# A two-layer mixture of experts behind a linear-attention scan: VectorE's order at five points, and gate products stored with the slot tile innermost

## The chip, the cores and the metric

The kernel runs on one core of a Trainium2 chip. The metric is device time in microseconds (us), the median of several executions; one further execution is profiled, and every row below comes from that one. The engines are named as in the profile: PE is TensorE (matmuls), PEld its weight loads, DVE is VectorE, ACT is ScalarE, POOL is GpSimd, SP only issues DMAs. A name with a q behind it (DVEq, ACTq) is that engine's sequencer, which handles waits, branches and register loads.

## What is computed

A gated linear recurrence over 4 x 768 positions gives a matrix x of 3072 tokens by 384. Two mixture-of-experts layers follow, both of this form (the second adds a bias per modality to the logits):

```python
logits = x @ w_gate
expert_idx = np.argmax(logits, axis=1)
probs = np.exp(logits - logits.max(-1, keepdims=True))
probs /= probs.sum(-1, keepdims=True) + 1e-09
gate_w = probs[np.arange(N), expert_idx]
for e in range(E):                      # 8 experts
    mask = expert_idx == e
    h = np.maximum(x[mask] @ w1[e], 0.0)          # 384 -> 1024
    out[mask] = gate_w[mask, None] * (h @ w2[e])  # 1024 -> 384
```

## The kernel before

After the attention the kernel works in two stages, one for each expert layer. The tokens are sorted by expert into slots of 128 tokens; a slot tile (below: a tile) is one such slot, and a stage has at most MT = 31 of them. In the profiled execution stage 1 runs tiles 0 to 26 and stage 2 runs tiles 0 to 24. Tiles from 24 on stand in branches that are taken only if the tile exists ("rest" branches); the first few tiles of each stage (2 and 4) are done ahead of the full table and end in a branch too.

One tile j is made of steps, each a closure with a name. For q = 0 to 3, `g1_q` is 18 matmuls of 128 columns (gathered tokens against a quarter of w1, each value split into a high and a low f16 part), `hh_q` is ACT's relu to f16, `hl_q` is DVE's low part (relu minus `hh_q`), and `g2_q` is 6 matmuls of 384 columns, of which every third needs `hl_q`. `ev` makes the output scale, `yo` is ACT's scaled output and POOL's scatter DMA. Beside them stand steps for later tiles: `sq` and `sv` scale the tokens of tile j+2 (ACT's square; then a chain of four DVE operations, L775 to L778, output `xs`), `T`, `xh`, `xl` transpose and split those of tile j+1, and in stage 1 `la` to `ld` make the logits of the second layer.

Where the expert changes, the new weights are split into f16 parts in place: ACT makes `wh` (L746), DVE `wl` (L747), in eight pieces of 128x768. A piece is named by h or l, the layer 0 or 1 and the quarter: `l11` is DVE's low part of w2's second quarter. Each stands in a branch that is taken where the expert changes; below, a tile where that happens is a split tile.

The order of all this is not left to a scheduler. A table POS gives every step of a tile a position (0 to 10, one number line for all engines), CHG does the same for the weight pieces (a position from 10 on means: in the next tile, 10 less), and EXT gives the steps that occur once per stage (position 23.74 is tile 2, 3.74). Steps are sorted by position and issued in that order, so each engine runs its instructions in the order of these numbers.

The routing is turned into slots by `finishing`, `tabling` and `gating`. `gating` (`gate1` and `gate2` in EXT, for the two stages) has four steps: ACT's exponential; DVE's sum, reciprocal, split of the gate into two f16 numbers and two products AQ = A x gate (A is the mask, 31 slot tiles by nt token tiles); on PE one matmul for each of the nt token tiles (24 in stage 1, 31 in stage 2) with AQ of that token tile as moving operand, 62 columns; and DVE's reading of the result, which gives each tile its scale and its token numbers.

Of the kernel before, what the change touches and what calls it, by code (L numbers as in the profile page):

```python
# [9 lines left out]
F16 = mybir.dt.float16  # L10
# [3 lines left out]
ALU = mybir.AluOpType  # L14
# [5 lines left out]
P = 128  # L20
# [5 lines left out]
NT = N // P  # L26
# [78 lines left out]
def attention(tc, ctx, C, q, k, v, a_re, a_im, wg, flags, emit_y, emit_lg, extra, ps, inp):  # L105
# [266 lines left out]
MT=31; MS=32; WF=544  # L372
# [4 lines left out]


POS=[dict(r1=-1.031,g1_0=0,hh_0=0.547,g1_1=0.882,hl_0=1.39,la=2.05,hh_1=2.196,g1_2=2.293,g2_0=2.443,lc=2.732,hl_1=3.114,r2=4.038,hh_2=4.156,T=4.338,
    g2_1=4.65,xh=4.8,hl_2=4.8,xl=5.173,sq=5.3,g1_3=5.65,hh_3=5.721,lb=5.802,g2_2=6.338,sv=6.511,lt=6.833,ga=6.883,ev=7.217,hl_3=7.445,ld=7.7,  # L380
    g2_3=8.105,yo=9.966),
    dict(la=-2.149,ga=-2.099,r1=-1.063,g1_0=-0.801,g1_1=-0.106,hh_0=1.2,hh_1=2.2,hl_0=2.367,hl_1=2.614,g1_2=2.928,T=3.282,r2=3.634,g2_0=3.64,lc=3.664,
    hh_2=4.688,xh=4.798,hl_2=4.8,xl=5.2,g1_3=5.366,sq=5.443,lb=5.487,g2_1=5.99,hh_3=6.083,hl_3=7.1,ev=7.3,g2_2=7.5,lt=7.586,ld=7.7,sv=7.978,g2_3=8.5,
# [4 lines left out]
    dict(h00=1.25,l00=2.555,h01=3.772,l01=3.889,h10=5,l10=5.85,h02=6.908,h11=7.334,l02=7.573,h03=8.381,l11=8.43,l03=9.238,h12=11.713,h13=12.469,l12=12.6,  # L388
    l13=13.5)]

EXT=dict(ga1=[9.894],tab1=[10.675,11.888,14.575,16.434,19.076],sc2=[14.852,16.409],tu2=[17.791,18.391,19.266],
    sc3=[16.942,20.231],gate1=[13.14,22.34,23.74,26.94],bias=[38.314],guess=[7.193,9.387],ec=[1.828,2.259,3.158],es=[5.811,7.12,9.347],eg0=[-0.314],
    eg1=[2.518],eg2=[2.797],eg3=[0.24],esc0=[7.854,8.86],esc1=[9.262,9.598],esc2=[17.6,18.2],esc3=[17.787,19.2],etu0=[10.7,10.819,11.2],etu1=[16.719,
    16.834,17.692],etu2=[20.882,21.035,21.741],etu3=[26.7,26.797,29.053],wsp=[0.41],lgl=[1.567,2.117,4.049,5.381,7.217],bat=[11.965,12.932,13.065,
    16.165],fin2=[15.779,17.6,18.5,21.1,21.3],ga2=[21.761],tab2=[18.791,23.611,24.661,26.111,28.111],scE=[31.762,31.857],tuE=[34.33,34.944,35.562],
    scF=[34.804,36.2],gate2=[33.763,38.234,40.083,40.999],ckw=[5.75,7.75],ck=[8.464])


HINT=1.5; DRAIN=6.9
# [33 lines left out]
class Router:  # L433
# [89 lines left out]
    def gating(s, pool, ps):  # L523

        tmp,sign,q,A,bm,T,gscale=s.late
        nc=s.tc.nc; C=s.C; nt=s.nt; nm=s.name
        K=lambda shape,n_,dt=F32: pool.tile(shape,dt,name=nm+n_,bufs=1)

        def once(f):
            def g(shape,n_,dt=F32):  # L530
                if n_ not in s.made: s.made[n_]=f(shape,n_,dt)
                return s.made[n_]
            return g
        K,T=once(K),once(T)
        sm,g2,dl,ig,iv=(T([P,w],n_) for n_,w in (("sm",nt),("g2",nt),("dl",nt),("ig",MT),("iv",MT))); mp=T([P,2*MT],"mp"); AQ=K([P,2,MT,nt],"AQ",F16)
        sg,val,ab=(K([P,MT],n_) for n_ in ("sg","val","ab")); ids=K([P,MT],"ids",I32)
        ex=T([P,nt,E],"ex"); nc.scalar.activation(ex,s.d,AF.Exp)
        yield
        g=s.gate; nc.vector.tensor_reduce(out=sm,in_=ex,op=ALU.add,axis=AX.X)
        nc.vector.tensor_scalar(out=sm,in0=sm,scalar1=1e-9,scalar2=None,op0=ALU.add)  # L540
        nc.vector.reciprocal(g,sm)
        if sign is not None:
            nc.vector.tensor_mul(g2,g,sign); g=g2
        nc.vector.tensor_copy(q[:,1,:],g)
        nc.vector.tensor_sub(dl,g,q[:,1,:])
        nc.vector.tensor_scalar(out=q[:,2,:],in0=dl,scalar1=1024.0,scalar2=None,op0=ALU.mult)
        for j in (1,2): nc.vector.tensor_tensor(out=AQ[:,j-1],in0=A,in1=bm(q[:,j,:]),op=ALU.mult)
        yield
        pm=ps.tile([P,512],F32,name="pm")
        for i in range(nt):  # L550
            nc.tensor.matmul(pm[:,:2*MT],s.boh[:,i,:],AQ[:,:,:,i],start=(i==0),stop=(i==nt-1))
        yield
        nc.vector.tensor_copy(mp,pm[:,:2*MT])
        s.sg,s.val,s.ab,s.ids=sg,val,ab,ids
        nc.vector.scalar_tensor_tensor(s.sg,mp[:,MT:],1.0/1024,mp[:,:MT],op0=ALU.mult,op1=ALU.add)
        nc.vector.tensor_scalar(out=s.val,in0=s.sg,scalar1=0.0,scalar2=None,op0=ALU.not_equal)
        if sign is not None: nc.scalar.activation(s.ab,s.sg,AF.Abs,scale=gscale)
        else: nc.vector.tensor_scalar(out=s.ab,in0=s.sg,scalar1=gscale,scalar2=None,op0=ALU.mult)
# [130 lines left out]
class Rot:  # L689
# [10 lines left out]
class Bufs:  # L700
# [48 lines left out]
class Stage:  # L749
# [98 lines left out]
    def tile(s, j, mid=(), old=None, chg=None, refill=False, **kw):  # L848


        W=s.W
        st=[(s.pos[k],f) for k,f in s.steps(j,**kw).items()]

        for k,p in s.chg.items():
            c=old if p>=10 else chg
            if c is None: continue
            def part(c=c,k=k):
                with s.tc.If(c["hl".index(k[0])]!=0): W.split(((int(k[1]),int(k[2])),),**{"lo" if k[0]=="h" else "hi":False})  # L858
            st.append((p%10,part))
        if refill:  # L860
            rf=s.refill(j-1)
            for k in ("r1","r2"): st.append((s.pos[k],lambda: next(rf)))
        st.extend(mid)
        st.sort(key=lambda t:t[0])
        for _,f in st: f()
# [194 lines left out]
def attention__moe__moe2_kernel(tc, q, k, v, a_re, a_im, w_gate, w1, w2, mid, w_gate2, mbias, out):  # L1060
    nc=tc.nc
    with ExitStack() as ctx:
# [8 lines left out]
        W=Weights(tc,cst)  # L1071
# [62 lines left out]
        with ExitStack() as mctx:  # L1134
# [31 lines left out]
            def logits(j, yo):  # L1166

                st=isinstance(j,int)
                px=rt.tile(); y=yo()
                for d in range(ND): nc.tensor.transpose(px[:,d*P:(d+1)*P],y[:,d*P:(d+1)*P],C.ident)  # L1170
                yield
                xT=bf.lxT.tile(); nc.scalar.copy(xT.rearrange("p d t -> p (d t)"),px[:,:DM])
                yield
                own=not st or j>=NL; pl=None
                if own:
                    pl=rt.tile()
                    for d in range(ND): nc.tensor.matmul(pl[:,:E],xT[:,d,:],wg2s[:,d,:],start=(d==0),stop=(d==ND-1))
                else:
                    xTs[j]=xT
                    if j%4==3: grp[0]=group(j-3)  # L1180
                p=(j-3)%4 if st and 3<=j<NL+3 else 3
                if p<3: next(grp[0])
                yield
                if p==0: next(grp[0])
                yield
                if own:
                    js=slice(j,j+1) if st else bass.ds(j,1)
                    nc.vector.tensor_tensor(out=R2.lg[:,js,:].rearrange("p o e -> p (o e)"),in0=pl[:,:E],in1=bias[:,js,:].rearrange("p o e -> p (o e)"),op=ALU.add)
                if p in (1,2): next(grp[0])
                elif st and p==3 and 3<j<NL+3: next(grp[0])  # L1190
                yield
# [6 lines left out]
            H1,H2={},{}  # L1198
            def put(H, nm, f, t=0):

                it=[]
                def step():
                    if not it: it.append(f())
                    next(it[0],0)
                for k in EXT[nm]:
                    j,k=divmod(k+.5,10); H.setdefault(t+int(j),[]).append((k-.5,step))
            def one(f):
                def g():
                    f(); yield
                return g  # L1210
# [9 lines left out]
            for i in range(EK):  # L1220
                put(H1,f"eg{i}",one(lambda i=i: S2.gather(i,exg[i],R2.eids[:,i:i+1])),EN+5)
                put(H1,f"esc{i}",lambda i=i: S2.scaling(i,eev[i],exs[i]),EN+5)
                put(H1,f"etu{i}",lambda i=i: S2.turning(i,exh[i],exl[i]),EN+5)
            put(H2,"wsp",one(lambda: W.split(((1,2),(1,3)))))
            put(H2,"lgl",lambda: logits(S1.last(),lambda: S1.ylast)); put(H2,"bat",lambda: R2.batch(NL,MT-NL,sb,rt,{},imv))
            put(H2,"fin2",lambda: R2.finishing(sb,sb,rt,1.0/(WS*WS),R1.idf))
            put(H2,"ga2",one(lambda: [S2.gather(EK+i) for i in range(3)]))
# [5 lines left out]
            ck=Check(tc,sb,cst,C,fl,W,R1,R2)  # L1233
# [97 lines left out]
```

## Time and profile before

| | |
|---|---|
| median of the timed executions | 791.32 us (790.51 to 792.84, 3 runs) |
| the profiled execution's own time | 784.05 us |
| its span, first to last instruction | 782.3 us |
| mean granted TensorE clock in it | 0.973 |
| PE busy | 730.2 us (93%) |
| DVE busy | 533.9 us (68%) |
| ACT busy | 474.5 us (61%) |
| POOL busy | 297.9 us (38%) |

Times in the rows are counted from the start of the span. A timeline row gives the start, the duration, the engine, the line, the operation, the tile that it writes and those that it reads, a count where rows are merged, and in square brackets how long the engine sat idle before it and who ended that. Matmuls overlap: a matmul row's duration includes the time in the pipeline, so the pace is read from the starts. The clock 1.00 is 2.4 GHz and 0.50 is 1.2 GHz.

### The profile page before, as it was taken

The numbers are of one execution on the slowest core, as the hardware profiler recorded it, in microseconds if no ns is written. First come the engines' busy times: TensorE is split into PE (matmuls) and PEld (weight loads), VectorE is DVE, ScalarE is ACT, GpSimd is POOL, SyncE is SP. The second block draws the span as 40 slices with busy tenths as digits, with TensorE's granted clock in tenths as the row PEclk, the third lists the DMA queues.
The fourth block names the chain that finished last, engine by engine and source line by source line (L and its number), as shares of the span: only waits on it lengthen the run. The fifth ranks groups of instructions, "written<-read, shape, count | busy, mean of one in ns | idle before, by whom it ended". The sixth has DMA issues, their size and how long they took to land. (4 is left out here: it accounts for less than half of the span.)

```text
span 782.3 us, 23431 instructions
## 1 busy us (share of the span) xinstructions
PE 730.2 (93%) x8451; PEld 587.4 (75%) x8451; DVE 533.9 (68%) x1415; ACT 474.5 (61%) x1007; POOL 297.9 (38%) x289
## 2 busy tenths in 40 slices
PE   7688999899899989999999999999899999999994
PEld 2367878787788867878777878788777878878873
DVE  7888898899789978474747586764564435445354
ACT  7799989798687426374746565675432436434452
POOL 5657788577575231222232224221121222222221
PEclk9799999899899999999999999999999999999997
DMA  9979777675231342433525162524033111611111
GB/s 211 221 146 214 174 153 165 118 173 102 62 82 62 98 158 79 165 112 126 165 91 176 61 197 82 194 68 170 19 112 125 59 47 43 222 43 43 63 42 30
DMA packets 159261, 91.40 MB, mean 117 GB/s; under 512 B 131804, under 2 KB 149764, under 8 KB 159104
## 3 DMA queue, kind: packets, MB, share of 16 engines
q1 hardware_dynamic: 151872, 68.49, 34.1%
q0 software_dynamic: 7232, 21.05, 8.8%
q8 instruction: 71, 1.16, 0.6%
q14 instruction: 86, 0.70, 0.3%
HBM read 192.54 MB, written 20.84 MB: 273 GB/s over the span
## 5 line engine op out<-in xcount | busy, mean ns | idle before, releaser
L823 PEld LDWEIGHTS <-wh 128*128 128x128 f16 x1296 | 127.6, 98 | 10.8 <-ACTq L888 3.0
L824 PEld LDWEIGHTS <-wh 128*128 128x128 f16 x1296 | 127.6, 98 | 8.2 <-issue 1.4
L825 PEld LDWEIGHTS <-wl 128*128 128x128 f16 x1296 | 127.6, 98 | 0.0
L844 POOL DMA_INDIRECT x<-yo,r1ids x27 | 31.7, 1174 | 181.8 <-ACT yo L843 125.0
L747 DVE SCALAR_TENSOR_TENSOR wl<-ws,wh 128x768 f16<-128x768 f32 x88 | 83.6, 962 | 13.1 <-ACTq L858 7.2
L746 ACT ACTIVATE wh<-ws 128x768 f16<-128x768 f32 x88 | 74.1, 844 | 8.9 <-ACTq L858 5.1
L836 PE MATMUL mpu<-wh,hl 128*128 128x384 f16 x216 | 70.5, 327 | 5.0 <-DVE hl L828 4.3
L836 PEld LDWEIGHTS <-hl 128*128 128x128 f16 x432 | 42.2, 98 | 42.3 <-DVE hl L828 11.8
L836 PE MATMUL mpy<-wh,hl 128*128 128x384 f16 x216 | 70.7, 327 | 2.5 <-DVE hl L828 1.6
L844 POOL DMA_INDIRECT out_dram<-yo,r2ids x21 | 21.0, 1002 | 130.9 <-ACT yo L843 123.8
L834 PE MATMUL mpy<-wh,hh 128*128 128x384 f16 x216 | 70.7, 327 | 0.0
L835 PE MATMUL mpy<-wl,hh 128*128 128x384 f16 x216 | 70.6, 327 | 0.0
L834 PE MATMUL mpu<-wh,hh 128*128 128x384 f16 x216 | 70.4, 326 | 0.0
L835 PE MATMUL mpu<-wl,hh 128*128 128x384 f16 x216 | 70.4, 326 | 0.0
L823 PE MATMUL mpk<-xh,wh 128*128 128x128 f16 x384 | 68.4, 220 | 1.3 <-ACTq L888 1.3
L823 PE MATMUL msc<-xh,wh 128*128 128x128 f16 x384 | 67.6, 219 | 1.3 <-DVEq L888 1.3
L825 PE MATMUL mpk<-xh,wl 128*128 128x128 f16 x384 | 68.4, 220 | 0.0
L824 PE MATMUL mpk<-xl,wh 128*128 128x128 f16 x384 | 68.4, 220 | 0.0
L825 PE MATMUL msc<-xh,wl 128*128 128x128 f16 x384 | 67.6, 219 | 0.0
L823 PE MATMUL mpq<-xh,wh 128*128 128x128 f16 x384 | 67.6, 219 | 0.0
L824 PE MATMUL mpq<-xl,wh 128*128 128x128 f16 x384 | 67.6, 219 | 0.0
L825 PE MATMUL mpq<-xh,wl 128*128 128x128 f16 x384 | 67.6, 219 | 0.0
(512 smaller groups left out, 2230.9 us busy)
## 6 DMA issues: line engine op xcount, KB each, us to landing
ws<-in_moe_w_dram SPq DMA_DIRECT2D x100, 1536.0 KB
ar<-in_a_re_dram SPq DMA_DIRECT2D x24, 192.0 KB
ai<-in_a_im_dram SPq DMA_DIRECT2D x24, 192.0 KB
k<-in_k_dram SPq DMA_DIRECT2D x24, 192.0 KB
q<-in_q_dram SPq DMA_DIRECT2D x24, 192.0 KB
v<-in_v_dram SPq DMA_DIRECT2D x24, 192.0 KB
x<-zero SPq DMA_DIRECT2D x8, 576.0 KB
x<-yt SPq DMA_DIRECT2D x24, 192.0 KB
```

What stands on the lines that cost most here:

```text
L746: nc.scalar.activation(H_,S_,AF.Copy,scale=WS,accum_out=s.fl[:,s.n:s.n+1]); s.n+=1
L747: if lo: nc.vector.scalar_tensor_tensor(L_,S_,WS,H_,op0=ALU.mult,op1=ALU.subtract)
L823: nc.tensor.matmul(o,W.h1[:,d,fs],x.h[:,d,:],start=(d==0),stop=False)
L824: nc.tensor.matmul(o,W.h1[:,d,fs],x.l[:,d,:],start=False,stop=False)
L825: nc.tensor.matmul(o,W.l1[:,d,fs],x.h[:,d,:],start=False,stop=(d==ND-1))
L834: nc.tensor.matmul(o,hh[:,r,:],W.h2[:,f,:],start=(f==0),stop=False)
L835: nc.tensor.matmul(o,hh[:,r,:],W.l2[:,f,:],start=False,stop=False)
L836: nc.tensor.matmul(o,hl[:,r,:],W.h2[:,f,:],start=False,stop=(f==NF-1))
L844: nc.gpsimd.indirect_dma_start(out=s.dst,out_offset=bass.IndirectOffsetOnAxis(ap=R.ids[:,j:j+1] if ids is None else ids(),axis=0),in_=y,in ...
```

## The change

Five points of the order are moved, and the layout of AQ is turned round. In stage 1 `hl_3` goes from 7.445 to 6.45, ahead of `sv` (6.511). The piece `l11` goes, in tiles from 23 on, to position 11.5, that is 1.5 of the next tile; its code for stage 2's first expert then stands in `wsp`, which also takes its two `wl` operations from 0.41 of stage 2's tile 0 to 2.7. The last two steps of stage 1's table (`tab1`) go from 16.434 and 19.076 to 15.6 and 16.42. The last three steps of stage 2's gates (`gate2`) go from 38.234, 40.083 and 40.999 to 42.65, 46.05 and 46.6, so out of tile 3 and the beginning of tile 4 into the middle of tile 4. AQ was stored as [2, 31, nt], the token tile innermost; it becomes [nt, 2, 31], so DVE writes it with a step of 62 elements, and each matmul reads 62 neighbouring elements.

```diff
...
-    g2_1=4.65,xh=4.8,hl_2=4.8,xl=5.173,sq=5.3,g1_3=5.65,hh_3=5.721,lb=5.802,g2_2=6.338,sv=6.511,lt=6.833,ga=6.883,ev=7.217,hl_3=7.445,ld=7.7,
+    g2_1=4.65,xh=4.8,hl_2=4.8,xl=5.173,sq=5.3,g1_3=5.65,hh_3=5.721,lb=5.802,g2_2=6.338,sv=6.511,lt=6.833,ga=6.883,ev=7.217,hl_3=6.45,ld=7.7,
...
+LATE=dict(l11=11.5)
...
-    scF=[34.804,36.2],gate2=[33.763,38.234,40.083,40.999],ckw=[5.75,7.75],ck=[8.464])
+    scF=[34.804,36.2],gate2=[33.763,42.65,46.05,46.6],ckw=[5.75,7.75],ck=[8.464])
...
-        sm,g2,dl,ig,iv=(T([P,w],n_) for n_,w in (("sm",nt),("g2",nt),("dl",nt),("ig",MT),("iv",MT))); mp=T([P,2*MT],"mp"); AQ=K([P,2,MT,nt],"AQ",F16)
+        sm,g2,dl,ig,iv=(T([P,w],n_) for n_,w in (("sm",nt),("g2",nt),("dl",nt),("ig",MT),("iv",MT))); mp=T([P,2*MT],"mp"); AQ=K([P,nt,2,MT],"AQ",F16)
...
-        for j in (1,2): nc.vector.tensor_tensor(out=AQ[:,j-1],in0=A,in1=bm(q[:,j,:]),op=ALU.mult)
+        for j in (1,2): nc.vector.tensor_tensor(out=AQ[:,:,j-1,:].rearrange("p n m -> p m n"),in0=A,in1=bm(q[:,j,:]),op=ALU.mult)
...
-            nc.tensor.matmul(pm[:,:2*MT],s.boh[:,i,:],AQ[:,:,:,i],start=(i==0),stop=(i==nt-1))
+            nc.tensor.matmul(pm[:,:2*MT],s.boh[:,i,:],AQ[:,i].rearrange("p a m -> p (a m)"),start=(i==0),stop=(i==nt-1))
...
-        for k,p in s.chg.items():
-            c=old if p>=10 else chg
-            if c is None: continue
...
+        when=lambda i,k: LATE.get(k,s.chg[k]) if i>=NT-1 else s.chg[k]
+        for k in s.chg:
+            for c,p in ((chg,when(j,k)),(old,when(j-1,k)-10)):
+                if c is None or not 0<=p<10: continue
...
-            put(H2,"wsp",one(lambda: W.split(((1,2),(1,3)))))
+            def rest():
+
+                W.split(((1,2),(1,3)),lo=False); W.split(((1,1),),hi=False)
+                yield
+                W.split(((1,2),(1,3)),hi=False)
+                yield
+            put(H2,"wsp",rest)
...
```

In the listings below the lines are those of each kernel: DVE's lines 747, 775 to 778, 828 and 840 of the kernel before are 749, 777 to 780, 830 and 842 of the changed one.

On DVE, in an ordinary split tile of stage 1 (tile 3), the last part of the tile before; `wl` is a weight piece, `ev` and `xs` the `sv` chain, the `ev` of line 840 the output scale, and `hl` the low part of the fourth quarter, `hl_3`:

```order
L747 SCALAR_TENSOR_TENSOR wl_113<-ws_91,wh_112 128x768
L858 UNCONDITIONAL_BRANCH x2
L775 TENSOR_SCALAR ev_4886<-fln 128x1
L776 TENSOR_SCALAR ev_4886<-ev_4886 128x1
L777 RECIPROCAL ev_4886<-ev_4886 128x1
L778 TENSOR_SCALAR xs_4017<-xg_4692,ev_4886 128x384
L840 TENSOR_TENSOR ev_4538<-ev_4538,r1ab 128x1
L858 UNCONDITIONAL_BRANCH x3
L828 SCALAR_TENSOR_TENSOR hl<-msc,hh 128x256
```

The same place in the changed kernel:

```order
L749 SCALAR_TENSOR_TENSOR wl_113<-ws_91,wh_112 128x768
L861 UNCONDITIONAL_BRANCH x5
L830 SCALAR_TENSOR_TENSOR hl<-msc,hh 128x256
L777 TENSOR_SCALAR ev_4887<-fln 128x1
L778 TENSOR_SCALAR ev_4887<-ev_4887 128x1
L779 RECIPROCAL ev_4887<-ev_4887 128x1
L780 TENSOR_SCALAR xs_4023<-xg_4693,ev_4887 128x384
L842 TENSOR_TENSOR ev_4538<-ev_4538,r1ab 128x1
```

`hl_3` has moved from behind the five small operations to in front of them.

On DVE, at the end of stage 1's tile 26, the last that exists, before; `r2lg` are logits of the second layer, the three `wl` are the pieces l02, l11 (`wl_113`) and l03, and L914 is the "rest" branch that is left here:

```order
L828 SCALAR_TENSOR_TENSOR hl<-mpk,hh 128x256
L858 COMPARE_AND_BRANCH
L747 SCALAR_TENSOR_TENSOR wl_111<-ws_90,wh_110 128x3x256
L858 UNCONDITIONAL_BRANCH x2
L1188 TENSOR_TENSOR r2lg<-mpT,bias 128x8
L858 COMPARE_AND_BRANCH
L747 SCALAR_TENSOR_TENSOR wl_113<-ws_91,wh_112 128x768
L858 UNCONDITIONAL_BRANCH x2
L858 COMPARE_AND_BRANCH
L747 SCALAR_TENSOR_TENSOR wl_111<-ws_90,wh_110 128x3x256
L858 UNCONDITIONAL_BRANCH x2
L914 COMPARE_AND_BRANCH
```

And in the changed kernel, where the branch is line 917:

```order
L861 COMPARE_AND_BRANCH
L749 SCALAR_TENSOR_TENSOR wl_111<-ws_90,wh_110 128x3x256
L861 UNCONDITIONAL_BRANCH x2
L1191 TENSOR_TENSOR r2lg<-mpT,bias 128x8
L861 COMPARE_AND_BRANCH
L749 SCALAR_TENSOR_TENSOR wl_111<-ws_90,wh_110 128x3x256
L861 UNCONDITIONAL_BRANCH x2
L917 COMPARE_AND_BRANCH
```

`l11` no longer stands ahead of the branch; it comes first in stage 2's tile 0, behind the branch.

On DVE, at the end of stage 2's tile 3, in front of the branch L888 that ends the tiles done ahead; `rfsm` to `rfq` and the two products `r2AQ` are the second step of `gate2`:

```order
L828 SCALAR_TENSOR_TENSOR hl<-mpq,hh 128x256
L840 TENSOR_TENSOR eev_3825<-eev_3825,r2eab 128x1
L539 TENSOR_REDUCE rfsm<-rfex 128x31
L540 TENSOR_SCALAR rfsm<-rfsm 128x31
L541 RECIPROCAL r2gate<-rfsm 128x31
L544 CAST rfq<-r2gate 128x31
L545 TENSOR_TENSOR rfdl<-r2gate,rfq 128x31
L546 TENSOR_SCALAR rfq<-rfdl 128x31
L547 TENSOR_TENSOR r2AQ<-rfA,rfq 128x961 x2
L687 TENSOR_LOAD r2tab
L888 COMPARE_AND_BRANCH
```

In the changed kernel they stand in tile 4, behind that branch, between `hl_1` (the `hl` that reads `mpq`) and `hl_2`:

```order
L830 SCALAR_TENSOR_TENSOR hl<-mpq,hh 128x256
L541 TENSOR_REDUCE rfsm<-rfex 128x31
L542 TENSOR_SCALAR rfsm<-rfsm 128x31
L543 RECIPROCAL r2gate<-rfsm 128x31
L546 CAST rfq<-r2gate 128x31
L547 TENSOR_TENSOR rfdl<-r2gate,rfq 128x31
L548 TENSOR_SCALAR rfq<-rfdl 128x31
L549 TENSOR_TENSOR r2AQ<-rfA,rfq 128x31x31
L861 UNCONDITIONAL_BRANCH
L549 TENSOR_TENSOR r2AQ<-rfA,rfq 128x31x31
```

The step has left the end of tile 3 for tile 4, and the products write a three-dimensional pattern. On PE the 31 matmuls of `gate2` move with them, from behind `g1_1` of tile 4 to behind its `g2_1`; on ACT and POOL the order of the work is unchanged.

## Rows read from the trace of the kernel before

**Rows 1.** Busy time by engine in stage 1 (us, instructions; last: PE clock, DMA)

```profile
270.00:560.00 290.00, 279.02 (x3345) 226.29 (x3343) 190.86 (x594) 162.27 (x415) 72.45 (x75) 0.99 0.39 129
```

**Rows 2.** PE's waits by who ended them: total us, times, longest

```profile
PE mpu L836 <- DVE hl L828: 4.3, 7, 1.6
...
PE mpq L823 <- DVEq L914: 1.9, 1, 1.9
...
PE mpk L823 <- ACTq L888: 1.3, 1, 1.3
```

**Rows 3.** Timeline of DVE, ACT and PE at the end of stage 1's tile 2

```profile
302.07 0.96 DVE L747 SCALAR_TENSOR_TENSOR wl<-ws,wh 128x768 f16<-128x768 f32 x1 [0.35 <-ACT wh L746]
...
302.63 0.39 ACT L827 ACTIVATE hh<-mpk 128x256 f16<-128x256 f32 x1
...
305.01 0.42 DVE L828 SCALAR_TENSOR_TENSOR hl<-mpk,hh 128x256 f16<-128x256 f32 x1
...
305.49 0.34 PE L836 MATMUL mpu<-wh,hl 128*128 128x384 f16 x1 [1.60 <-DVE hl L828]
```

**Rows 4.** Timeline of DVE and PE across the end of a split tile

```profile
339.22 0.95 DVE L747 SCALAR_TENSOR_TENSOR wl<-ws,wh 128x768 f16<-128x768 f32 x1
...
341.54 0.34 PE L836 MATMUL mpu<-wh,hl 128*128 128x384 f16 x1 [0.40 <-DVE hl L828]
...
343.05 1.83 DVE L747 SCALAR_TENSOR_TENSOR wl<-ws,wh 128x768 f16<-128x768 f32 x2
...
345.87 0.33 PE L836 MATMUL mpy<-wh,hl 128*128 128x384 f16 x1
```

**Rows 5.** Timeline of DVE, ACT and PE from stage 1 to stage 2

```profile
550.04 1.82 DVE L747 SCALAR_TENSOR_TENSOR wl<-ws,wh 128x768 f16<-128x768 f32 x2
...
550.15 0.58 ACT L843 ACTIVATE yo<-mpu,ev 128x384 f32<-128x384 f32 x1 [0.18 <-ACT wh L746]
...
551.97 0.22 PE L823 MATMUL mpq<-exh,wh 128*128 128x128 f16 x1 [1.91 <-DVEq L914]
```

**Rows 6.** Four short stretches: PE, PEld, DVE, ACT, POOL busy; PE clock

```profile
552.40:555.70 3.30, 3.30 (x34) 3.30 (x32) 2.16 (x3) 1.76 (x5) 0.34 (x1) 0.50 0.10 38
...
591.33:592.33 1.00, 1.00 (x18) 0.99 (x18) 0.00 (x0) 0.00 (x0) 0.78 (x1) 1.00 0.60 211
593.30:596.70 3.40, 3.40 (x36) 3.40 (x34) 0.00 (x0) 0.38 (x1) 0.99 (x1) 1.00 0.01 5
596.80:600.10 3.30, 3.30 (x25) 2.76 (x23) 2.45 (x11) 0.96 (x3) 0.00 (x0) 0.50 0.23 60
```

**Rows 7.** The gates' products and matmuls, slot matmuls: ns min/median/max, first to last start

```profile
L551 PE MATMUL mpT<-r2AQ,r2boh x31: 268/284/287, 593.3 to 596.5; 128*128 128x62 f16 x31
...
L551 PE MATMUL mpT<-r1AQ,r1boh x24: 270/289/291, 297.5 to 300.0; 128*128 128x62 f16 x24
...
L547 DVE TENSOR_TENSOR r1AQ<-rfA,rfq x2: 537/538/539, 296.4 to 296.9; 128x744 f16<-128x744 f16 x2
L547 DVE TENSOR_TENSOR r2AQ<-rfA,rfq x2: 670/672/674, 590.0 to 590.6; 128x961 f16<-128x961 f16 x2
...
L516 PE MATMUL mpt<-rfA,r2boh x31: 213/233/235, 573.2 to 574.9; 128*128 128x31 f16 x31
```

**Rows 8.** Timeline of PE: a block of matmuls with neighbouring columns

```profile
565.48 0.42 PE L470 MATMUL mpt<-r2oh,ones 128*128 128x80 bf16 x10
565.76 0.20 PE L471 MATMUL mpt<-r2acc,ones 128*128 128x88 bf16 x1
```

**Rows 9.** Timeline of DVE, ACT and PE from stage 2's tile 3 to 4

```profile
588.39 0.41 DVE L539 TENSOR_REDUCE rfsm<-rfex 128x31 f32<-128x248 f32 x1
...
589.97 1.26 DVE L547 TENSOR_TENSOR r2AQ<-rfA,rfq 128x961 f16<-128x961 f16 x2
...
590.51 0.19 ACT L843 ACTIVATION_READ_ACCUMULATOR eyo<-mpu,eev 128x1 f32 x1
...
591.33 0.22 PE L823 MATMUL msc<-xh,wh 128*128 128x128 f16 x1 [1.34 <-DVEq L888]
```

More of the change, by code (lines that the diff above doesn't have):

```diff
@@ L389 @@
     l13=13.5)]
-EXT=dict(ga1=[9.894],tab1=[10.675,11.888,14.575,16.434,19.076],sc2=[14.852,16.409],tu2=[17.791,18.391,19.266],
+LATE=dict(l11=11.5)
+EXT=dict(ga1=[9.894],tab1=[10.675,11.888,14.575,15.6,16.42],sc2=[14.852,16.409],tu2=[17.791,18.391,19.266],
     sc3=[16.942,20.231],gate1=[13.14,22.34,23.74,26.94],bias=[38.314],guess=[7.193,9.387],ec=[1.828,2.259,3.158],es=[5.811,7.12,9.347],eg0=[-0.314],
     eg1=[2.518],eg2=[2.797],eg3=[0.24],esc0=[7.854,8.86],esc1=[9.262,9.598],esc2=[17.6,18.2],esc3=[17.787,19.2],etu0=[10.7,10.819,11.2],etu1=[16.719,
-    16.834,17.692],etu2=[20.882,21.035,21.741],etu3=[26.7,26.797,29.053],wsp=[0.41],lgl=[1.567,2.117,4.049,5.381,7.217],bat=[11.965,12.932,13.065,
+    16.834,17.692],etu2=[20.882,21.035,21.741],etu3=[26.7,26.797,29.053],wsp=[0.41,2.7],lgl=[1.567,2.117,4.049,5.381,7.217],bat=[11.965,12.932,13.065,
     16.165],fin2=[15.779,17.6,18.5,21.1,21.3],ga2=[21.761],tab2=[18.791,23.611,24.661,26.111,28.111],scE=[31.762,31.857],tuE=[34.33,34.944,35.562],
-    scF=[34.804,36.2],gate2=[33.763,38.234,40.083,40.999],ckw=[5.75,7.75],ck=[8.464])
+    scF=[34.804,36.2],gate2=[33.763,42.65,46.05,46.6],ckw=[5.75,7.75],ck=[8.464])
 HINT=1.5; DRAIN=6.9
@@ L852, in tile, with part @@
         st=[(s.pos[k],f) for k,f in s.steps(j,**kw).items()]
-        for k,p in s.chg.items():
-            c=old if p>=10 else chg
-            if c is None: continue
-            def part(c=c,k=k):
-                with s.tc.If(c["hl".index(k[0])]!=0): W.split(((int(k[1]),int(k[2])),),**{"lo" if k[0]=="h" else "hi":False})
-            st.append((p%10,part))
+        when=lambda i,k: LATE.get(k,s.chg[k]) if i>=NT-1 else s.chg[k]
+        for k in s.chg:
+            for c,p in ((chg,when(j,k)),(old,when(j-1,k)-10)):
+                if c is None or not 0<=p<10: continue
+                def part(c=c,k=k):
+                    with s.tc.If(c["hl".index(k[0])]!=0): W.split(((int(k[1]),int(k[2])),),**{"lo" if k[0]=="h" else "hi":False})
+                st.append((p,part))
         if refill:
```

## The prediction, made before the changed kernel ran

> **What bounds the kernel.** I read the share of each engine first: PE is busy for 93% of the span, and in stage 1 for 279.0 of 290 us, DVE for 226 and ACT for 191 [rows 1]. So in the experts' part the time is PE's work plus its idle time, and only these two can be shortened. Next I read PE's waits: 4.3 us in 7 waits are for an `hl` of DVE, 1.9 and 1.3 twice over are branches (the engine after which PE goes on is DVE's or ACT's sequencer) [rows 2, 9]. Then I read the timeline round each of these waits, to see what DVE did while PE stood, and last the granted clock of short stretches: two of 3.3 us ran at 0.50, that is at 1.2 GHz, one right behind the 1.91 us of idle between the stages, one right behind the 31 matmuls of stage 2's gates [rows 5, 6].
>
> All sums are made against the profiled execution's own 784.05 us (1.75 outside its span). The median of the timed runs is 791.32, 7.3 us above it; I carry the difference over.
>
> **1. `hl_3` ahead of `sv`.** At the end of tile 2 DVE is done with `wl` at 303.03 and ACT with `hh_3` at 303.02, but `hl_3` starts only at 305.01, and PE, which waits for nothing else, resumes at 305.49 after 1.60 us idle [rows 3]. In between stand the `sv` chain, the last step of stage 1's gates and the `ev` of line 840. With the step at 6.45, `hl_3` runs from 303.03 to 303.45, before PE runs dry at 305.49 - 1.60 = 303.89: this wait ends. What moves behind `hl_3` is 0.42 us later: the tokens' scale for tile j+2 (not due for a tile), the output scale and with it `yo` (its buffer is due a tile later), the next `wl`. The last could be felt in a split tile: two pieces run from 343.05 to 344.88, then comes the next tile's `hl_0`, which at 0.42 is done at about 345.3; PE takes it at 345.87, so there is some 0.5 of slack [rows 4], and the 0.40 idle at 341.54 is gained. Not all 4.3 can be: a PE that arrives earlier finds the next tile's first `hh` and `hl` no earlier, where these wait for ACT or for the pieces. I take four fifths, **-3.4**; bounds -1.5 (the first 1.60 alone, the rest met by later waits) and -4.3.
>
> **2. Stage 1's table steps earlier.** They are some small DVE operations each and end inside tile 1. PE's 1.3 us wait there is ended by ACT's branch [rows 2], which stays behind ACT's own `yo`. I take **0**, from -0.3 to +0.4 (casts now ahead of an `hl_3`, which would then be late by their own time, at most one 0.42).
>
> **3. `l11` and `wsp`.** PE's 1.91 us between the stages end with DVE's branch, and DVE's last work there is two `wl` of together 1.82 us, to 551.86 [rows 5]. Without `l11` DVE is done one piece (0.95 us, [rows 4]) earlier, at about 550.9. ACT's `yo`, done at 550.73, is next late. So the idle falls from 1.9 to 1.0: **-0.9**, no more than -1.1. In stage 2's tile 0 the order is `l11` first, as late as before, then `hl_0`; the two other pieces now come at 2.7, behind `hl_0` and `hl_1`, for a quarter of w2 that is used at the end of the tile. I take nothing for these.
>
> Behind that idle PE ran 3.3 us at 0.50 [rows 6]. At full clock the same work takes half: **-1.7** if an idle of 1.0 does not bring the fall. Tile 4 of stage 2 starts after 1.34 us idle at 1.00 [rows 6, 9], which speaks for it.
>
> **4. AQ's layout, stage 1.** DVE: the two products of 744 elements take 538 ns each, 0.72 ns per element [rows 7]. Written with a step of 62 elements (124 bytes) they leave whatever makes them that fast. No strided store stands in the trace; the nearest rows are DVE's plain f32 passes, 768 elements in 0.95 us and 256 in 0.42, that is 1.035 ns for each further element [rows 3, 4], so 0.925 for 744: +0.39 each, **+0.8** for the pair; PE waits for the second. From below: 0 (the store is free). From above, the only strided accesses that I can read are PE's (the matmuls below): 62 columns in 104 ns are 1.7 ns per column; at that price a product takes 1.30, +1.5 for the pair.
>
> The Trainium skill, "VectorE: DVE Perf Modes", section "What auto-detection actually checks", has VectorE's doubled mode only where every tensor is 16-bit with a step of one, so the edit would lose it; that the products before run at 0.72 ns agrees. Its figure of one element per cycle gives, as an estimate, 932 ns for a product of stage 1, so +0.8 for the pair too.
>
> PE: with a column step of nt elements the 24 matmuls start over 2.5 us, 104 ns apart, in stage 2 31 over 3.2 us; slot matmuls of 31 such columns start 55 ns apart (1.7 over 31) [rows 7]. Both give 1.7 to 1.8 ns per column. Ten matmuls of 8 to 80 neighbouring columns start 28 ns apart [rows 8], and 18 of 128 columns take 1.00 us, 56 each [rows 6]. For 62 neighbouring columns I take 31 ns, near the former: 24 x 31 = 0.75 for 2.5, **-1.8**. Bounds: 56 ns (-1.2) and 104 ns (0). Stage 1's gates together: -1.0.
>
> **5. `gate2` out of tile 3, and the layout there.** At the end of tile 3 DVE's chain runs from 588.39 to 591.23 and PE idles for 1.34 until DVE's branch; ACT's last instruction before it ends at 590.70 [rows 9]. Without the chain DVE is early and ACT decides: **-0.4**. The 31 matmuls go from 3.2 to 31 x 0.031 = 0.95: **-2.2** (56 ns: -1.5; 104: 0). The products (672 ns for 961 elements, [rows 7]) cost by the same slope 0.95 + 193 x 1.035 ns = 1.15 each, +1.0 for the pair, but in the middle of tile 4 that lies beside PE's matmuls as far as the tile reaches. PE gets to the gate matmuls behind four blocks of 18 (1.00 each, [rows 6]), two `g2` steps of about as much and three transposes, so 6.1 to 6.6 after the tile's start. On DVE `hl_1` ends about 3.0 after it (two blocks, `hh_1` at 0.39 and `hl_1` at 0.42 [rows 3], and some 0.2 between them); the six small operations take 589.97 - 588.39 = 1.58 [rows 9] and the products 2.3, to 6.9: 0.3 to 0.8 late, I take 0.5. Then `hl_3` stands behind the step that reads the result, some 0.4 more: **+0.9** (0 to 2.0).
>
> The second half-clock stretch, 596.8 to 600.1, comes right behind the block of gate matmuls, in which PE idled for nothing [rows 6]: 3.4 us of slow issue with PE reckoned busy. If the block is 0.95, I expect no fall: **-1.7**.
>
> The Trainium skill, "Advanced Engine Details and Errata", section "Memory Cachelines", says that an access to another 16-byte line each time is penalised. For PE's reads the trace agrees (1.7 ns per column at steps of 48 and 62 bytes); what it would do to DVE's stores at 124 bytes is not shown here.
>
> **What costs nothing.** No DMA is added, removed or made of other bytes; ACT's and POOL's orders stay, SP reads its registers in another order at two refills, a tile ahead of need. DVE's added work, 0.8 + 1.0, is small beside its 64 us idle in stage 1 [rows 1].
>
> **Sum.** -3.4 + 0 - 0.9 - 1.7 - 1.0 - 0.4 - 2.2 + 0.9 - 1.7 = -10.4, so 773.7 for the profiled execution. The two clock terms (3.4) are one execution's and may be absent from others; I count half, -8.7, which on the median of 791.32 gives **782.5**.
>
> **Rivals.**
> (a) DVE's strided stores cost as much as PE's strided reads, 1.7 to 1.75 ns per element: 1.30 and 1.68 us a product, +0.7 in stage 1 and +1.1 in stage 2 over my sum: 784.3. For it: the reads' price; against: DVE's f32 passes move twice the bytes at 1.035. Chance 0.14.
> (b) The gains are given back: PE, earlier by `hl_3`, waits for the next tile's `hh` and `hl` instead (+3.4), and the clock still falls (+1.7): 787.6. For it: split tiles keep DVE and ACT almost full; against: the slack in [rows 4]. Chance 0.13.
> (c) The layout doesn't do what it says: the pace of these matmuls is set by something else, such as their 128x128 weights, and stays at 104 ns. Then +4.0 with the half clock's share +0.9: 787.4. Against: 18 matmuls, each with its own weights, take 56 each [rows 6]. Chance 0.06.
> (d) Slower: the stores are so dear that PE waits for them. 1488 elements in stage 1 hold PE directly, 1922 in stage 2 beyond the slack above. Above about 1.035 + 8.7/3410 us = 3.6 ns per element the gain is gone, and from about 4.3 (another 2.4 us) the kernel is slower; at 5 ns it is 782.5 + 3.97 x 3.41 = 796. Nothing in the trace costs DVE that much. Chance 0.05.
>
> **Chances and range.** The main case has 0.60 (0.02 is left for what I don't see). Its own range is 779 to 785, from the bounds of terms 1, 4 and 5; the range that holds 8 of 10 takes in (a), (b) and (c): 777 (all clock terms, `hl_3` in full, one more) to 788.5. About 0.3%, 2.4 us, is what a measurement of this kernel can tell from no change: faster by more than that in the main case, (a) and (c) and nearly always in (b), together 0.87; within it 0.07; slower 0.06.
>
> **What the profile after would show.** Step 1: no wait of PE for `hl` over 0.5 us at the ends of stage 1's tiles, `hl_3` directly behind `wl` or as soon as `hh_3` is there; wrong, if the 4.3 stands again under another line. Step 3: about 1.0 idle between the stages, ended by ACT or DVE at 0.9 past the last piece, and a clock near 1.00 behind it. Step 4: products of 0.9 to 1.0 and 1.1 to 1.2 us, gate matmuls some 30 ns apart, PE's wait before stage 1's longer by 0.8. Step 5: about 0.9 idle at the end of tile 3, no wait over 0.6 in tile 4, no half clock behind the gate matmuls. The prediction is wrong if the products take over 2 us, if the matmuls stay above 56 ns, or if stage 1's PE time falls by less than 1.5 us.

## The result, and the profile after

The changed kernel takes 797.92 us (median of 11), the kernel before, run beside it, 792.0 (11): ratio 1.0072, 95% interval 1.005 to 1.0094, so 0.7% slower. The prediction, 782.5 in 777 to 788.5, had the wrong sign. The profiled execution has a span of 795.3 us, and with the 1.8 outside it lies near its median. That of the kernel before (784.05) lay 5 us below the fastest of its timed ones; a second profiled execution of it, used below, took 790.76.

First the products and the gates' matmuls, as [rows 7] had them. The columns are nanoseconds (least, median, most), first and last start, and the form:

```profile
L549 DVE TENSOR_TENSOR r1AQ<-rfA,rfq x2: 3472/3576/3680, 296.7 to 299.7; 128x744 f16<-128x744 f16 x2
L549 DVE TENSOR_TENSOR r2AQ<-rfA,rfq x2: 4448/4550/4653, 604.4 to 608.4; 128x961 f16<-128x961 f16 x2
...
L553 PE MATMUL mpT<-r2AQ,r2boh x31: 208/237/240, 613.1 to 614.7; 128*128 128x62 f16 x31
...
L553 PE MATMUL mpT<-r1AQ,r1boh x24: 233/237/240, 303.5 to 304.7; 128*128 128x62 f16 x24
```

A product of 744 elements took 538 ns and now takes 3576, one of 961 took 672 and now 4550: 4.8 and 4.7 ns per element. PE's waits, as in [rows 2], show who pays (total, times, longest):

```profile
PE mpT L553 <- DVEq L861: 6.9, 1, 6.9
...
PE mpT L553 <- DVE r1AQ L549: 5.7, 1, 5.7
...
PE mpT L1308 <- DVE ckout L1274: 3.2, 1, 3.2
...
PE mpq L825 <- DVEq L917: 1.5, 1, 1.5
```

The two largest waits of the experts' part stand in front of the two blocks of gate matmuls. The first, in stage 1, is ended by the product itself. The second is put down to DVE's sequencer, but nothing but the two products runs on DVE from 604.37 to 613.09:

```profile
604.28 0.18 DVE L548 TENSOR_SCALAR rfq<-rfdl 128x31 f16<-128x31 f32 x1
604.37 8.72 DVE L549 TENSOR_TENSOR r2AQ<-rfA,rfq 128x961 f16<-128x961 f16 x2
```

The idle time costs a second time. Six stretches, with busy time of PE, PEld, DVE, ACT, POOL, then PE's clock: each wait, the block of gate matmuls behind it, and what follows.

```profile
297.45:303.45 6.00, 0.28 (x2) 0.00 (x0) 6.00 (x3) 1.14 (x4) 0.00 (x0) 0.73 0.00 1
303.47:304.70 1.23, 1.23 (x24) 1.23 (x25) 1.23 (x3) 0.00 (x0) 0.00 (x0) 0.50 0.00 0
304.70:308.00 3.30, 3.30 (x28) 2.33 (x26) 2.54 (x4) 1.89 (x5) 0.00 (x0) 0.64 0.01 2
606.00:613.10 7.10, 0.24 (x2) 0.01 (x1) 7.09 (x2) 0.00 (x0) 3.18 (x1) 0.84 0.10 28
613.14:614.75 1.61, 1.60 (x32) 1.60 (x32) 0.89 (x2) 0.00 (x0) 0.00 (x0) 0.50 0.00 0
614.80:618.10 3.30, 3.30 (x14) 1.61 (x12) 2.38 (x13) 0.00 (x0) 0.00 (x0) 0.56 0.02 5
```

Both blocks ran wholly at 0.50 (1.2 GHz), so the matmuls stand 51 and 52 ns apart (1.23 us over 24, 1.61 over 31) where I had 31; the next 3.3 us ran at 0.64 and 0.56.

### The profile page after: what moved, and what is told of

It is laid out like the page before. It is cut to its first block, busy times and chain, and to the rows that moved or that the text cites. A ratio compares the mean times of both kernels' runs of the same rounds, so it can differ in the third digit from the quotient of the medians.

```text
span 795.3 us, 23426 instructions
## 1 busy us (share of the span) xinstructions
PE 732.2 (92%) x8451; PEld 583.0 (73%) x8451; DVE 546.0 (69%) x1415; ACT 470.2 (59%) x1007; POOL 296.3 (37%) x289
## 5 line engine op out<-in xcount | busy, mean ns | idle before, releaser
L846 POOL DMA_INDIRECT x<-yo,r1ids x27 | 28.5, 1054 | 195.9 <-ACT hh L829 93.6
L830 DVE SCALAR_TENSOR_TENSOR hl<-mpq,hh 128x256 f16<-128x256 f32 x73 | 30.9, 423 | 56.0 <-ACTq L861 22.9
L826 PE MATMUL msc<-xl,wh 128*128 128x128 f16 x384 | 67.6, 219 | 0.0
```

The costliest lines, as they stand in the source:

```text
L826: nc.tensor.matmul(o,W.h1[:,d,fs],x.l[:,d,:],start=False,stop=False)
L830: def hl(q=q): nc.vector.scalar_tensor_tensor(hs[q][2],hs[q][0][:,:,:P],0.0,hs[q][1],op0=ALU.max,op1=ALU.subtract)
L846: nc.gpsimd.indirect_dma_start(out=s.dst,out_offset=bass.IndirectOffsetOnAxis(ap=R.ids[:,j:j+1] if ids is None else ids(),axis=0),in_=y,in ...
```

## The experiments

Every time is a median; the interval is that of the ratio to the kernel before, run on the same chip. Each run has 4 to 12 executions, but `e5_store_prices` and `e6_before_again` a single one. In the diffs only the changed part of a long line is shown.

**The parts alone.** `e1_five_points` has the moved points and AQ as before:

```diff
-AQ=K([P,nt,2,MT],"AQ",F16)
+AQ=K([P,2,MT,nt],"AQ",F16)
...
-nc.vector.tensor_tensor(out=AQ[:,:,j-1,:].rearrange("p n m -> p m n"),in0=A,in1=bm(q[:,j,:]),op=ALU.mult)
+nc.vector.tensor_tensor(out=AQ[:,j-1],in0=A,in1=bm(q[:,j,:]),op=ALU.mult)
...
```

> The five moved points without the layout: AQ stored as before, [2, 31, nt]. Theory S (the strided store explains the loss: in the changed kernel the products take 3.58 and 4.55 us each, 4.7 to 4.8 ns per element, PE idles 6.1 and 7.2 us in front of the two blocks of gate matmuls, and the blocks themselves give back 1.25 and 1.5): taking those out of 797.9 leaves 797.9 - 6.0 + 1.25 - 7.2 + 1.5 = 787.5, about 0.6% faster than before. Theory O (the moved points lose on their own account, since the changed kernel's trace shows some 5 us more of stage 1 beside the gates): 794 or more, no faster than before. By my prediction's terms for the points alone (-3.4, -0.9, -1.7, -0.4 and half of the clock): 786 to 788.

Measured: 786.36, ratio 0.9941 (0.9923 to 0.9959). Theory S holds, O falls.

`e2_layout_only` is the kernel before with the diff's three AQ lines and none of the moved points.

> The kernel before with the layout alone. Theory S: the stage 1 products are 5 us longer with PE waiting, stage 2's 7.8 longer at the end of tile 3, where the branch holds PE; the blocks give back 1.25 and 1.6: 792 + 4.8 + 6.2 = 803, 1.3% slower. Theory O: the layout is the smaller part, under 797.

Measured: 802.0, ratio 1.0138 (1.0124 to 1.0153). In its trace the products take 3574 and 4550 ns, and the waits stand where theory S put them:

```profile
PE msc L823 <- DVEq L888: 8.8, 1, 8.8
...
PE mpT L551 <- DVE r1AQ L547: 5.8, 1, 5.8
```

The layout loses 10.7 us on the kernel before (802.0 against 791.34); in the changed kernel, where the points gain 5.0, it loses 11.6 (797.92 against 786.36, each from its own group of runs).

**Which access is dear.** `e3_store_rows` walks the same products token tile by token tile:

```diff
-nc.vector.tensor_tensor(out=AQ[:,:,j-1,:].rearrange("p n m -> p m n"),in0=A,in1=bm(q[:,j,:]),op=ALU.mult)
+nc.vector.tensor_tensor(out=AQ[:,:,j-1,:],in0=A.rearrange("p m n -> p n m"),in1=q[:,j,:].unsqueeze(2).to_broadcast([P,nt,MT]),op=ALU.mult)
```

> The changed kernel with the products walked token tile by token tile: the store is of 31 neighbours, and the mask A is read with a step of nt elements (48 and 62 bytes) instead. If it is the store with a step that costs (S1), a product falls from 3.58 to about 0.8 to 1.3 us and from 4.55 to 1.0 to 1.7, PE's two long waits go, and the time is 784 to 788. If DVE pays the same for a read with a step (S2), the products stay at 3.5 and 4.5 us and the time at 797 to 798.

Measured: 786.02, ratio 0.9945 (0.9927 to 0.9963). AQ lies in memory as in the changed kernel; only the walk differs, so that the mask is read with a step and nothing is stored with one. The products take 1448 and 1779 ns, 1.9 ns per element: S1, though they are a little dearer than the 1.3 and 1.7 us that I had given it at most.

`e4_token_rows` turns the mask round too, so that nothing has a step:

```diff
...
-big=T([P,2,MT,nt],"A",F16) if two is None else two(); A=big[:,0]; AQ=big[:,1]
-bm=lambda x: x.unsqueeze(1).to_broadcast([P,MT,nt])
+big=T([P,2,nt,MT],"A",F16) if two is None else two(); A=big[:,0]; AQ=big[:,1]
+bm=lambda x: x.unsqueeze(2).to_broadcast([P,nt,MT])
...
-s.boh[:,i,:],AQ[:,:,i]
+s.boh[:,i,:],AQ[:,i,:]
...
-nc.vector.tensor_tensor(out=AQ[:,:,j-1,:].rearrange("p n m -> p m n"),in0=A,in1=bm(q[:,j,:]),op=ALU.mult)
+nc.vector.tensor_tensor(out=AQ[:,:,j-1,:],in0=A,in1=bm(q[:,j,:]),op=ALU.mult)
...
```

> The changed kernel with the mask A too stored as [nt, 31], so that the products read and write neighbours, and the 31-column slot matmuls read neighbours as well. S1 and S2 both: products of 0.8 to 1.0 and 1.0 to 1.2 us (no doubled pace, since the gate is now repeated along the innermost walk), gate matmuls 52 ns apart, slot matmuls below 55, PE's long waits gone: 783 to 787, the fastest of the four. Theory O: 794 or more, since the points stay as in the changed kernel.

Measured: 782.13, ratio 0.9891 (0.9877 to 0.9905), the fastest kernel of the study and a little below the 783 to 787 that I had expected. Its products (busy time, mean ns of one, idle before):

```profile
L549 DVE TENSOR_TENSOR r2AQ<-rfA,rfq 128x961 f16<-128x961 f16 x2 | 2.2, 1152 | 0.0
L549 DVE TENSOR_TENSOR r1AQ<-rfA,rfq 128x744 f16<-128x744 f16 x2 | 1.8, 928 | 0.0
```

and the stretch of its stage 1 block of gate matmuls:

```profile
296.14:296.87 0.73, 0.73 (x24) 0.73 (x25) 0.73 (x2) 0.11 (x1) 0.00 (x0) 1.00 0.01 4
```

These are the prices I had predicted for the changed kernel: 1.15 and 0.925 us a product, 31 ns a matmul (0.73 us over 24 is 30), at clock 1.00. My expectation of 52 ns for this run was wrong: 52 was the pace at the half clock.

`e5_store_prices` measures the disputed cost by itself, with products on scratch at the end of the kernel before:

```diff
+for st,w in ((1,1),(2,1),(4,2),(8,4),(16,8),(31,15),(32,16),(62,31),(64,31)):
+    n,v=ways(f[:,:961] if st==1 else f,st,w); c=A[:,:n].rearrange("p (s a) -> p s a",s=w)
+    V.tensor_tensor(out=v,in0=c,in1=c,op=ALU.mult)
...
```

`ways` gives a view whose inner walk has a step of `st` elements.

> The kernel before with 19 products and 4 fills on scratch added to DVE at the very end, behind everything that the output needs; their durations are the result, the kernel's time is some 40 us longer. Stores of some 960 f16 values at steps of 1, 2, 4, 8, 16, 31, 32, 62 and 64 elements (2 to 128 bytes): if the price belongs to the step in bytes, it rises with the step and is flat from some step on, about 4.7 ns per element at 62; if it belongs to f16 stores that are not neighbours (each a part of a word), it is there from a step of 2 on. Reads at 2, 8, 32 and 62 elements tell whether reads pay it too; f32 stores at 1, 2, 4, 16, 31 and 32 elements tell whether the type matters: 1.04 ns each if only two-byte stores are dear.

The f16 stores, each alone in a stretch; steps 1, 2, 4, 8, 16, 31, 32, 62, 64, with 961, 961, 960, 960, 960, 930, 960, 961 and 930 elements (the third number is DVE's busy time in us):

```profile
789.22:789.90 0.68, 0.67 (x1) 0.50 0.00 0
789.91:791.15 1.24, 1.23 (x1) 0.50 0.00 0
791.18:793.47 2.29, 2.29 (x1) 0.50 0.00 0
793.50:797.91 4.41, 4.41 (x1) 0.50 0.00 0
797.94:802.12 4.18, 4.17 (x1) 0.50 0.00 0
802.15:806.34 4.19, 4.18 (x1) 0.50 0.00 0
806.36:810.70 4.34, 4.33 (x1) 0.50 0.00 0
810.72:815.16 4.44, 4.43 (x1) 0.50 0.00 0
815.19:819.49 4.30, 4.30 (x1) 0.50 0.00 0
```

Per element: 0.70, 1.28, 2.4, 4.6 ns at steps of 2, 4, 8 and 16 bytes, and 4.3 to 4.6 from there on. Neither of my two guesses was right alone: the price is there from a step of 2 on, and it doubles with the step until 16 bytes. Reads with a step of 2 and of 8 elements, then f32 stores at 1, 2, 4 and 16 (544, then 272 elements each):

```profile
819.52:820.70 1.18, 1.17 (x1) 0.50 0.00 0
820.72:822.58 1.86, 1.84 (x1) 0.50 0.00 0
...
826.17:826.90 0.73, 0.71 (x1) 0.50 0.00 0
826.92:827.38 0.46, 0.44 (x1) 0.50 0.00 0
827.40:828.05 0.65, 0.64 (x1) 0.50 0.00 0
828.07:828.70 0.63, 0.62 (x1) 0.50 0.00 0
```

A read with a step costs 1.2 and 1.9 ns per element, and at 32 elements still 1.8. An f32 store costs 1.3, 1.6, 2.4 and 2.3: flat from 16 bytes on as well, at half the f16 price.

**The moved points.** `e6_before_again` is the kernel before, profiled once more.

> The kernel before, profiled once more, since its profiled execution (784.05) lies 5 us under every timed one. If the stretch from stage 1's first full tile to stage 2 takes again 259 us, the 5 us that the changed kernel's stage 1 is longer beside its gates belong to the moved points; if it takes 263 to 265, they belong to the execution, and the two traces can't be compared for them.

Measured: 790.76 in one run. From the first full tile to stage 2 it takes 266.7 us (291.42 to 558.11), the first profile of before 259.3: the traces of two executions of one kernel differ by more than what the points are worth, and below I compare with this second profile. Its `hl` waits are 6.8 us in 7, where [rows 2] had 4.3. And the 3.3 us behind `gate2`'s matmuls, at 0.50 in [rows 6], ran at 1.00 here:

```profile
603.20:606.50 3.30, 3.26 (x45) 2.60 (x43) 2.81 (x11) 1.37 (x4) 0.81 (x1) 1.00 0.22 60
```

`e7_hl3_only` has `hl_3=6.45` and nothing else.

> The kernel before with hl_3 alone moved. As my term had it: PE's waits for hl at the ends of stage 1's tiles (6.8 us in 7 in the second profile of before) go and come back nowhere: -3.4 or more, 787 to 788 against 791.3. If they are given back (the five-points trace has about 1.4 us less in stage 1 only, with new waits of 0.5 to 0.8 on hl, hh and xs in split tiles): 790 to 791.

Measured: 790.85, ratio 1.0 (0.9979 to 1.0022). PE's waits in stage 1, of the second profile of before:

```profile
PE mpu L836 <- DVE hl L828: 6.6, 6, 1.6
PE mpL L788 <- DVEq L858: 2.2, 1, 2.2
PE mpy L836 <- DVE hl L828: 1.6, 3, 0.9
```

and with `hl_3` moved:

```profile
PE mpL L788 <- DVEq L858: 3.8, 1, 3.8
PE mpy L836 <- DVE hl L828: 1.4, 4, 0.5
PE mpu L836 <- DVE ev L775: 0.9, 4, 0.2
PE mpt L1170 <- ACT yo L843: 0.9, 2, 0.6
PE mpt L571 <- DVE guess L627: 0.6, 1, 0.6
PE mpu L834 <- ACT hh L827: 0.6, 1, 0.6
```

The waits at the tile ends are gone as forecast. In their place stand 1.6 us more in front of the transposes of stage 2's first tokens (`mpL`, which PE now reaches earlier), and small waits for `ev`, `yo`, `guess` and `hh`, together 3.0 (0.2 before): of 6.8 us, 4.4 are back, and 0.4 more at the boundary between the stages, where PE now idles for 2.3 us instead of 1.9. What is left did not shorten the stage: from the first full tile to stage 2 it takes 268.1 us here and 266.7 in the second profile of before, with PE busy for 256.5 and 253.6 us of it. Why PE was busy longer is not shown. The timed runs, 12 against 35, show no gain; their interval leaves room for at most 1.7 us.

`e8_l11_only` has the late `l11` and the two-step `wsp`, with `hl_3`, `tab1` and `gate2` as before.

> The kernel before with l11 and wsp alone moved. Boundary between the stages: one wl fewer ahead of the branch, -0.4 to -0.9, and the half clock behind it gone, -1.7. If the shorter end too (6.4 us from the last g2 matmul to the final check's matmul in before, 3.9 with the five points) comes from l11, whose branch then no longer stands in the last tile of stage 2: another -2.5, so 786.5 to 787.5 against 791.3. If not: 789.

Measured: 787.21, ratio 0.9945 (0.9924 to 0.9966): as much as all five points. PE's idle time between the stages is 0.9 us shorter (1.9 to 1.0). The clock behind it, second profile of before, then `e1_five_points`:

```profile
558.50:561.80 3.30, 3.30 (x35) 3.30 (x34) 2.16 (x3) 1.86 (x5) 0.38 (x1) 0.55 0.10 38
```

```profile
557.60:560.90 3.30, 3.30 (x55) 3.16 (x53) 1.79 (x4) 2.82 (x8) 0.33 (x1) 1.00 0.11 41
```

0.55 after 1.9 us of idle, 1.00 after 1.5; 55 matmuls where 35 were. But the length of the idle time does not decide this by itself. In `e7_hl3_only`, where `l11` stands as before, PE idled for 2.3 us and ran at 1.00 behind it:

```profile
557.94 0.22 PE L823 MATMUL mpq<-exh,wh 128*128 128x128 f16 x1 [2.30 <-DVEq L914]
...
558.33:561.63 3.30, 3.30 (x56) 3.15 (x54) 2.39 (x4) 2.61 (x8) 0.00 (x0) 1.00 0.10 38
```

Over all profiles the clock there was 0.50 to 0.59 in the five with both `hl_3` and `l11` in their old places, and 1.00 in the nine with at least one of them moved.

The end is shorter too. DVE's idle in front of the first instruction behind the last branch, in `e8_l11_only`:

```profile
781.87 0.18 DVE L1305 TENSOR_SCALAR_CACHE_REDUCE ckb<-fly 128x31 f32<-128x31 f32 x1 [1.57 <-DVEq L917]
```

and in `e10_no_gate2`:

```profile
784.26 0.18 DVE L1305 TENSOR_SCALAR_CACHE_REDUCE ckb<-fly 128x31 f32<-128x31 f32 x1 [4.90 <-DVEq L917]
```

`e9_late_stage1` and `e10_no_gate2` undo one thing each of the five points:

```diff
-LATE.get(k,s.chg[k]) if i>=NT-1 else
+LATE.get(k,s.chg[k]) if i>=NT-1 and s.logits is not None else
...
-gate2=[33.763,42.65,46.05,46.6]
+gate2=[33.763,38.234,40.083,40.999]
```

> The five points, but l11's late place only in stage 1; in stage 2 it stands at 8.43 as before. If the shorter end comes from that place in stage 2: about 6.4 us again from the last g2 matmul to the final check's matmul, 786.4 + 2.5 = 788.9. If it comes from something else: 3.9 us and 786.4.

Measured: 788.57, ratio 0.9972 (0.9951 to 0.9993).

> The five points without gate2's move: products and chain again at the end of stage 2's tile 3. My term for the move alone, with the old layout, is -0.4 at the branch: 786.8. If the move of the 31 matmuls into tile 4 makes new waits behind them, leaving it out is no slower: 785.5 to 786.4.

Measured: 789.62, ratio 0.997 (0.9951 to 0.999). Both are slower than `e1_five_points`, by 2.2 and 3.3 us (2.4 and 2.3 by the ratios, each uncertain by some 2), and in both the idle behind the last branch is long again (5.33 and 4.90 us). It is 4.3 to 5.3 in eight profiles (both of before, `e2_layout_only`, `e5_store_prices`, `e7_hl3_only`, `e9_late_stage1`, `e10_no_gate2`, `e11_token_rows_only`) and 1.55 to 1.57 in six (the changed kernel, `e1_five_points`, `e3_store_rows`, `e4_token_rows`, `e8_l11_only`, `e12_token_rows_no_hl3`), though DVE's instructions around the branch are the same in all but `e5_store_prices`. So `l11`'s place in stage 2 was not the cause that `e9_late_stage1` was to show, since `e10_no_gate2` has it and is long. What decides between the two is open. The 14 profiles suggest that it goes by the program, not by the execution, but only the kernel before was profiled twice (4.50 and 4.63). One candidate that no run tests is code that arrives late behind the branch: during this idle time the two DMA queues that the profile names "instruction" start 4 to 6 transfers in the eight long profiles, and 2 or 3 in the six short ones. Of the 3.3 us that `gate2`'s move seems worth, 2.8 stand there (6.7 us instead of 3.9 between PE's last two starts), and in `e10_no_gate2` the 3.3 us behind the gate matmuls ran at 0.56, so the move itself is worth nothing that can be measured.

**The layout without the points, and the points without `hl_3`.** `e11_token_rows_only` is the kernel before with the layout of `e4_token_rows`; `e12_token_rows_no_hl3` is `e4_token_rows` with `hl_3` and `tab1` where they were.

> The kernel before with mask and products both stored with the slot tile innermost, and walked in that order; no point of the order moved. If the layout itself gains once no store has a step: what it gave on top of the five points (786.4 to 782.1, -4.2), less about 1 us because the dearer products (1.15 for 0.67 us each) stand in front of the branch at the end of tile 3: 787 to 789 against 791.4. If the gain hangs on the moved points: 790 to 792.

Measured: 790.98, ratio 0.9993 (0.9974 to 1.0011): no gain, against my expectation. The trace has the dearer products in three places, since the mask's own two passes lose their pace as well (931 and 1165 ns):

```profile
PE mpt L516 <- DVE rfA L512: 2.7, 2, 1.4
PE msc L823 <- DVEq L888: 2.3, 1, 2.3
...
PE mpT L551 <- ACT wh L746: 0.8, 1, 0.8
```

2.7 us where it was 1.1, 2.3 where it was 1.3, 0.8 where nothing was. Together these waits are 3.4 us longer, against blocks of gate and slot matmuls that are some 5.5 us shorter (2.5 to 0.7, 3.2 to 1.1, 1.3 to 0.6 and 1.7 to 0.8). So most of the matmuls' gain is spent; where the rest went is not shown.

> Mask and products with the slot tile innermost, l11, wsp and gate2 moved, but hl_3 and tab1 left where they were before. If moving hl_3 is worth nothing, as it was alone (790.85 against 791.51): 781 to 783, no different from 782.1 with it. If it is worth my term: 785.5.

Measured: 784.6, ratio 0.9915 (0.9897 to 0.9934). That is between the two values that I had named. `e4_token_rows` is faster by 2.5 us between the medians and by 1.9 between the ratios, and the intervals touch: in these surroundings `hl_3` and `tab1` may be worth about 2 us, or nearly nothing; alone, `hl_3` was worth none that could be measured.

## Why the prediction was wrong

**The step that failed** is the price of AQ's store in parts 4 and 5: "1.035 ns for each further element", with an upper end of 1.75. I took DVE's store with a step for an ordinary unpacked pass, with PE's reads with a step as the worst case. Measured: 4.8 and 4.7 ns in the kernel, 4.6 in `e5_store_prices`. The price was the rival (d), at 5 ns, with a chance of 0.05 and "Nothing in the trace costs DVE that much"; no row that I had read stored with a step either, so that sentence excluded nothing. Products of over 2 us are also the first sign of being wrong that the prediction names. The rows that I had read held f16 stores of neighbours only, and reads are no bound for stores: `e3_store_rows` shows 1.9 ns for the one and the changed kernel 4.7 for the other.

By its steps, from 782.5: PE stands in front of the gate matmuls for 6.0 us in stage 1, 5.2 more than my 0.8, and for 7.1 in stage 2, 6.6 more than my 0.5 (the lengths of the two stretches above; the idle times that the profile gives are 5.7 and 6.9): +11.8. The blocks at 0.50 take 1.23 and 1.61 instead of 0.75 and 0.95: +1.1. What follows them at 0.64 and 0.56 costs up to 3.3 x 0.36 + 3.3 x 0.44 = 2.6. The two clock terms, of which I had counted half, cancel: one came in full, one not at all. `hl_3`, -0.7 instead of -3.4 (the medians of `e7_hl3_only` and its own before; by their ratio 0): +2.7. The end, which I had not looked at: -2.7 (3.5 for 6.3 us between the last two starts on PE). Together 798, against 797.9; the agreement to a tenth is luck, since the terms come from single executions and this account was made after the result.

**Right:** the matmuls over neighbouring columns (30 ns in `e4_token_rows`); the price of a product without the doubled pace (928 and 1152 ns there, where nothing is stored with a step but the gate is repeated along the innermost walk), and with it PE's waits in front of the gate matmuls, 0.8 and 0.4 us there where I had 0.8 and 0.5; the branch at the end of tile 3 (0.9 us of idle in the changed kernel); the idle time between the stages (1.0 us in `e8_l11_only`), and a full -1.7 rather than half for the clock behind it, though `e7_hl3_only` shows that the shorter idle time is not the whole reason; `tab1` and the DMAs at nothing, as far as the runs tell (`tab1` was never moved by itself).

**Right by luck:** the order without the layout, 786 to 788 by my terms and 786.36 measured. `hl_3` did not give its 3.4, and some 2.7 us came from the end, for which I had no term.

**Right in mechanism, not in size:** `hl_3`, whose waits went as foreseen but came back behind it, as rival (b) said. Some of them came back between the stages: PE idles there for 1.5 us in the changed kernel, in which both are moved, and for 1.0 in the two kernels that move `l11` without `hl_3`. **Not reliably there to gain:** the half clock behind `gate2` [rows 6]. With the gates' old order and layout that stretch ran at 0.50 and 0.56 in two profiles (the first of before, `e10_no_gate2`) and at 1.00 in four (`e5_store_prices`, `e6_before_again`, `e7_hl3_only`, `e8_l11_only`).

**Misread, without weight in the sum:** in [rows 1] the second busy time is that of PE's weight loads. DVE was busy for 191 us and ACT for 162, not 226 and 191, so DVE idled for 99 us, not 64. And 791.32 - 8.7 is 782.6, not 782.5.

The Trainium skill's "Memory Cachelines" ("Advanced Engine Details and Errata") names lines of 16 bytes and a penalty for another line at each access. The prices that go flat at a step of 16 bytes agree with the line's size. It also asks for at least two accesses to a line to absorb the memory's latency. F16 stores with a step of 8 bytes make two, and they cost 2.4 ns per element here against 0.70 for neighbours, so on these stores two were not enough.

## What to carry to other kernels

Where the innermost walk of a DVE instruction decides between a store and a read with a step, let the read have it (1.9 ns per element, the store 4.7), or turn the source round as well and have neither (1.2), if the passes that make the source can bear it: in `e11_token_rows_only` they lost their pace too, and the kernel gained nothing. A price that no row shows is not bounded by rows of another engine or of the other direction: give the rival that rests on it a chance to match, above all where PE waits directly. An idle PE pays twice here: after 6 to 7 us of waiting the next 4.5 to 5 us ran at 0.50 to 0.64 of the clock. After 2.3 us in `e7_hl3_only` they did not.

## What was not expected of the hardware

A store of f16 with a step costs DVE twice an f32 store at 16 bytes and more (4.3 to 4.6 and 2.3 ns per element). And one branch at the end of the program cost 4.3 to 5.3 us of DVE's time in eight profiles and 1.6 in six; some 3 us of the comparisons in this study hang on it, and the cause stays open.
